# Second matmul and transposes as two 64-row array tiles, the upper half of each sum 1.5 steps behind the lower one

## The chip, the cores and the metric

One core of a Trainium2 chip runs the kernel. The metric is the device time of one execution in microseconds. The kernel before took 799.05 us (median of three runs, 798.12 to 799.97). Engine names are those of the profile: PE is the matrix engine and PEld its weight loads, DVE the vector engine, ACT the scalar engine, POOL and SP the two that issue transfers here.

## What is computed

A lightweight causal convolution (each of 8 heads has 7 softmax weights over time) is followed by a two-layer network with a leaky ReLU. Cut to what matters:

```python
# x: (8, 4096, 192)   weight: (8, 7)   w_in: (192, 2048)   w_out: (2048, 192)
w = softmax(weight, axis=-1)
y[b, s, c] = sum_k w[head(c), k] * x_padded[b, s + k, c]     # 6 zeros ahead of each row
h = y.reshape(32768, 192) @ w_in
g = maximum(0.01 * h, h)
out = g @ w_out                                              # (32768, 192), float32
```

## The kernel before, in words

**Tiling.** The 8 batch rows are taken in pairs. A *block* is 512 tokens of both rows of a pair, so there are 32 blocks (`NBLK`), and a block is worked on in 8 *steps* (`STEPS`). Two blocks are a *unit*, the piece that the convolution works on. The 192 channels are three chunks of 64 (`NCH`, `CH`); the two rows of a pair stand on partitions 0 to 63 and 64 to 127 of the same tiles.

**The stages of a block.** SP loads x; DVE casts it to bf16 (`cast_x`, L86); PE transposes it in 12 full 128x128 transposes (`transpose_x`, L98) into one tile `ptr` of two PSUM banks; DVE copies that out in one operation (`evac_x`, L110); the convolution is 21 DVE operations per unit (`conv_jobs`, L130 and L136), kept in the list `jobs` and handed out a few per step. The first matmul (`mm1`, L238) makes one tile `ph` of hidden values for each of 16 slices `f`: six pairs of matmuls over 64 rows and 512 columns, in each pair one on the lower and one on the upper 64 rows of the array, one batch row each. ACT turns each `ph` into bf16 hidden values `g` (L245). The second matmul (`mm2`, L256) adds 16 matmuls over all 128 rows and 192 columns into one sum for 128 tokens; two sums share a tile `po`, and DVE copies both out at once (`evac_o`, L268) for SP to store.

**What sets the order.** The order is written by hand (`manual_schedule`), and every engine runs its own list in that order. Step j of block b issues two `mm1` (12 matmuls, two ACT operations) and then the sum j of block b-1 (16 matmuls): the second matmul runs one block behind the first. At block b the steps j = 0, 1, 2 also cast, transpose and copy out x of block b+3. The convolution of unit u+1 is handed out while unit u is multiplied, from step 3 of the unit's first block on, two operations a step. The PSUM tiles are `ph` twice (two banks each), `po` twice (one bank each) and `ptr` once (two banks); the hidden values `g` have two buffers, the output tiles `o_sb` four.

**Names below.** A *pair* is two 64-row matmuls, one on the lower 64 rows of the array and one on the upper. An *even* block is the first of its unit (0, 2, 4 and so on).

## Time and profile before

| what | value |
|---|---|
| median of three runs | 799.05 us |
| the profiled execution, its own time | 798.81 us |
| its span, first to last instruction | 797.0 us |
| PE busy | 759.1 us, 95% |
| DVE, ACT busy | 517.2 us (65%), 506.6 us (64%) |
| first `mm2` matmul, last PE matmul ends | 57.03 us, 792.72 us |
| mean granted TensorE clock | 0.980 |

How to read it: the span is 1.8 us shorter than the execution's own time. A matmul's row gives its start and a length that overlaps the next one's, so the rate at which PE works is read from the distance of starts, not from the lengths. In the timeline a row is a run of equal instructions: its start, how long the run lasted, the engine, the line, the operation, how many, and in brackets the idle time before it with what ended that.

### The profile page before, as it was taken

To read this page: it belongs to the slowest core of one execution; us is meant where nothing else is said; L and a number is where in the kernel's file an instruction comes from. 1 tells how busy PE (TensorE), PEld (TensorE's weight loads), DVE (VectorE), ACT (ScalarE), POOL (GpSimd) and SP (SyncE) were. 2 spreads that over 40 slices of the span, in tenths; PEclk is the share of its full clock that TensorE was granted. 3 is DMA by queue.
4 is the path that set the end of the run, shared out by engine and by line. 5 is a ranking of instruction groups with operands and counts; after the bars stand their busy time and mean duration, and the time that the engine had idled before them with its cause. 6 is when DMAs were issued, how large, how long until landed. Compare 5 with 4: busy or idle time off the path is not lost.

```text
span 797.0 us, 16911 instructions
## 1 busy us (share of the span) xinstructions
PE 759.1 (95%) x7612; PEld 486.5 (61%) x7612; DVE 517.2 (65%) x592; ACT 506.6 (64%) x521; POOL 8.4 (1%) x19
## 2 busy tenths in 40 slices
PE   3299899999999999999999999999999999999997
PEld 3146566666666666666666666666666666666666
DVE  3889594766939476693947669394766939476011
ACT  1586466666666666666666666666666666666661
POOL 4000000000000000000000000000000000000000
PEclk9589899999999999999999999999999999999999
DMA  8910222212222211222221122222122221111111
GB/s 206 266 43 30 69 72 73 60 49 80 71 75 76 71 53 58 80 71 71 79 71 53 59 80 71 71 80 71 46 66 80 71 71 40 31 40 31 41 31 61
DMA packets 70097, 56.16 MB, mean 70 GB/s; under 512 B 3752, under 2 KB 69304, under 8 KB 69640
## 3 DMA queue, kind: packets, MB, share of 16 engines
q1 hardware_dynamic: 68608, 50.34, 20.9%
q0 software_dynamic: 1104, 4.73, 2.6%
q8 instruction: 59, 0.97, 0.5%
q14 instruction: 14, 0.11, 0.1%
q10 hardware_dynamic: 312, 0.01, 0.0%
HBM read 29.90 MB, written 25.17 MB: 69 GB/s over the span
## 4 chain that ended last, share of the span: by engine, by line
PE 89%; DVE 5%; DMA 3%; ACT 1%; issue 1%; POOL 0%; ACTq 0%; POOLq 0%
PE po L256 44%; PE ph L238 43%; DVE yt L136 4%; DMA w_stage<-in_moe_w_in_dram 3%; PE ptr L98 2%; ACT w_in L217 1%; DMA wk<-in_weight_dram 1%; DVE xt L110 0%; DVE o_sb L268 0%; DVE x_bf L86 0%; DVE yt L130 0%; ACT g L245 0%; POOL wk L156 0%; POOL w_stage L167 0%; POOL ident masks.py:199 0%
## 5 line engine op out<-in xcount | busy, mean ns | idle before, releaser
L245 ACT ACTIVATE g<-ph 128x1024 bf16<-128x1024 f32 x512 | 496.4, 1021 | 248.2 <-PE ph L238 248.1
L256 PEld LDWEIGHTS <-g 128*128 128x128 bf16 x4096 | 326.2, 98 | 105.8 <-issue 105.6
L238 PE MATMUL ph<-yt,w_in 64*128 64x512 bf16 x3072 | 381.5, 381 | 8.3 <-DVE yt L136 4.1
L256 PE MATMUL po<-w_out,g 128*128 128x192 bf16 x4096 | 382.2, 247 | 0.0
L136 DVE SCALAR_TENSOR_TENSOR yt<-xt,wk,yt 128x1024 bf16<-128x1024 bf16 (+1 forms) x306 | 373.4, 1220 | 8.7
L238 PEld LDWEIGHTS <-w_in 64*128 64x128 bf16 x3072 | 130.4, 94 | 173.5 <-issue 51.4
L268 DVE COPY o_sb<-po 128x384 f32<-128x384 f32 x128 | 71.1, 556 | 247.8 <-PE po L256 247.8
L98 PE MATMUL ptr<-ident,x_bf 128*128 128x128 bf16 x384 | 27.9, 225 | 17.1 <-DVE x_bf L86 17.1
L98 PEld LDWEIGHTS <-x_bf 128*128 128x128 bf16 x384 | 24.5, 101 | 18.5 <-DVE x_bf L86 17.2
L110 DVE COPY xt<-ptr 128x1536 bf16<-128x1536 bf16 x32 | 30.4, 951 | 7.4 <-PE ptr L98 5.8
L86 DVE CAST x_bf<-x_nat 128x768 bf16<-128x768 f32 x64 | 32.6, 552 | 0.0
L130 DVE TENSOR_SCALAR yt<-xt,wk 128x1024 bf16<-128x1024 bf16 (+1 forms) x51 | 23.7, 465 | 0.5
L217 ACT CAST w_in<-w_stage 128x1536 bf16<-128x1536 f32 x4 | 5.6, 1468 | 17.6 <-DMA w_stage<-in_moe_w_in_dram 17.6
L179 PE MATMUL warm<-ident 128*128 128x128 bf16 x60 | 6.0, 295 | 8.3 <-POOL ident masks.py:199 8.3
L179 PEld LDWEIGHTS <-ident 128*128 128x128 bf16 x60 | 5.8, 141 | 8.3 <-POOL ident masks.py:199 8.3
L187 DVE TENSOR_REDUCE nmax<-wk 128x3 f32<-128x21 f32 x1 | 0.2, 176 | 10.7 <-DMA wk<-in_weight_dram 10.7
L192 ACT ACT_TABLE_LOAD x1 | 1.3, 1283 | 7.8 <-DMA wk<-in_weight_dram 7.8
L156 POOL DMA_DIRECT2D wk<-in_weight_dram x10 | 5.3, 537 | 1.9 <-DMA wk<-in_weight_dram 1.1
L222 ACT CAST w_out<-wo_stage 128x3072 bf16<-128x3072 f32 x1 | 2.7, 2748 | 0.0
L192 ACT ACTIVATE wk<-wk,nmax 128x7 f32<-128x7 f32 x3 | 0.8, 302 | 1.8 <-DVE nmax L187 1.8
L167 POOL DMA_DIRECT2D w_stage<-in_moe_w_in_dram x2 | 1.3, 646 | 0.0
L172 POOL DMA_DIRECT2D wo_stage<-in_moe_w_out_dram x1 | 1.2, 1196 | 0.0
(11 smaller groups left out, 2.2 us busy)
## 6 DMA issues: line engine op xcount, KB each, us to landing
x_nat<-in_x_dram SPq DMA_DIRECT2D x64, 384.0 KB, 4.3
out_dram<-o_sb SPq DMA_DIRECT2D x128, 192.0 KB, 2.0
w_stage<-in_moe_w_in_dram POOLq DMA_DIRECT2D x2, 1536.0 KB, 16.9
wo_stage<-in_moe_w_out_dram POOLq DMA_DIRECT2D x1, 1536.0 KB, 25.3
wk<-in_weight_dram ACTq DMA_DIRECT2D x6, 0.7 KB
wk<-in_weight_dram POOLq DMA_DIRECT2D x6, 0.7 KB, 4.5
wk<-in_weight_dram ACTq DMA_DIRECT2D x2, 0.4 KB, 4.4
wk<-in_weight_dram ACTq DMA_DIRECT2D x2, 0.2 KB
```

The costliest lines, as they stand in the source:

```text
L86: nc.vector.tensor_copy(out=t[:, :, :, e, :], in_=x_nat[blk][:, e, :, :].rearrange("p s (c k) -> p s c k", c=NCH),)
L98: nc.tensor.transpose(out=t[:, c, s, :], in_=x_bf[blk][:, s, c, :, :].rearrange("p e k -> p (e k)"), identity=ident,)
L110: nc.vector.tensor_copy(out=xt[rp][:, :, HALO + st * ST : HALO + (st + 1) * ST], in_=ptr[blk][:, 0:NCH, :, :].rearrange("p c s t -> p c (s ...
L130: lambda s=src, d=dst, c=c: nc.vector.tensor_scalar_mul(d, s, wk[:, c, 0:1])
L136: lambda s=src, d=dst, c=c, k=k: nc.vector.scalar_tensor_tensor(out=d, in0=s, scalar=wk[:, c, k : k + 1], in1=d, op0=mybir.AluOpType.mult, ...
L156: eng.dma_start(out=wk[p : p + hi - lo, c, :], in_=weight[h : h + 1, :].to_broadcast((hi - lo, K)),)
L179: nc.tensor.matmul(out=wa[:, 0, 0:128], lhsT=ident, rhs=ident, start=(i == 0), stop=(i == 59),)
L217: nc.scalar.copy(out=w_in[:, :, q * (F // 4) : (q + 1) * (F // 4)], in_=w_stage[:, :, q * (F // 4) : (q + 1) * (F // 4)],)
L238: nc.tensor.matmul(out=ph[:, e, :], lhsT=w_in[ps, c, f * 128 : (f + 1) * 128], rhs=y[ps, c, ub * ST : (ub + 1) * ST], start=(c == 0), stop ...
L245: nc.scalar.activation(out=g[blk][:, f, :, :], in_=ph, func=mybir.ActivationFunctionType.Prelu, alpha=0.01,)
L256: nc.tensor.matmul(out=p[:, j % 2, :], lhsT=g[blk][:, fc, e, s * 128 : (s + 1) * 128], rhs=w_out[:, fc, :], start=(fc == 0), stop=(fc == N ...
L268: nc.vector.tensor_copy(out=o_sb, in_=po.pop((blk, q)))
```

## The change

The second matmul becomes pairs too. Each sum is split over the contraction: the lower 64 rows of `g` and `w_out` add 16 matmuls of 192 columns, the upper 64 rows another 16, and both halves add into the same `po` tile, which is now one sum wide and has a bank of its own. In step n the lower half of sum n is issued, alternating with upper-half matmuls that lag by `LAG` = 24 matmuls: first the last eight of sum n-2, then the first eight of sum n-1. A sum is therefore finished in the middle of the step two after its own, and is copied out there (`evac_o` with one sum of 192 columns instead of two). The first upper-half matmul of a sum is made to wait for the first ACT operation of the same step (`seal`). The last nine sums (from `LAST` on) are still made with 128 rows; before them come 24 upper-half matmuls without a partner.

The transposes become 24 transposes of 64 rows, alternating between the array's halves, into two tiles `ptr0` and `ptr1`. These and the `po` tiles now share one pool of four banks. `evac_x` is two copies. `g` has three buffers. The preparation of x runs one block further ahead (block b+4) at the steps 1 and 2, with the copies out right after the transposes and one convolution operation between; block 1 prepares two blocks. The convolution operations are spread evenly over the steps from step 0 of an even block.

PE where `mm1` ends and the second matmul begins; before (`ph` hidden values before ACT, `po` sums, `g` hidden values):

```order
L238 LDWEIGHTS w_in_255
L238 MATMUL ph_1511<-yt_927,w_in_255 128x512
L256 LDWEIGHTS g_1074
L256 MATMUL po_1485<-w_out_260,g_1074 128x192
L256 LDWEIGHTS g_1074
```

and now:

```order
L242 LDWEIGHTS w_in_280
L242 MATMUL ph_1448<-yt_511,w_in_280 128x512
L260 LDWEIGHTS g_982
L260 MATMUL po_1456<-w_out_285,g_982 128x192 [waits DVE_49]
L260 LDWEIGHTS g_515
L260 MATMUL po_1351<-w_out_285,g_515 128x192
```

The matmuls of two sums, from two blocks' hidden values here, now alternate, and the first of a new sum waits for DVE to have emptied its bank. In the middle of the same step the upper half changes over to the next sum:

```order
L260 LDWEIGHTS g_515
L260 MATMUL po_1351<-w_out_285,g_515 128x192
L260 LDWEIGHTS g_982
L260 MATMUL po_1456<-w_out_285,g_982 128x192
L260 LDWEIGHTS g_515 [waits Activation_49]
L260 MATMUL po_1403<-w_out_285,g_515 128x192
```

That weight load carries the new wait for ACT; nothing like it stood there before.

PE where the transposes begin in an even block; before:

```order
L256 LDWEIGHTS g_3204
L256 MATMUL po_3528<-w_out_260,g_3204 128x192
L98 LDWEIGHTS x_bf_3548 [waits DVE_49]
L98 MATMUL ptr_3585<-ident_114,x_bf_3548 128x128
L98 LDWEIGHTS x_bf_3548
```

and now:

```order
L260 LDWEIGHTS g_4165
L260 MATMUL po_4687<-w_out_285,g_4165 128x192
L101 LDWEIGHTS x_bf_4725 [waits DVE_49]
L101 MATMUL ptr0_4781<-ident_111,x_bf_4725 128x64
L101 LDWEIGHTS x_bf_4725
L101 MATMUL ptr1_4782<-ident_111,x_bf_4725 128x64 [waits DVE_49]
```

The first wait is for the cast, as before. The second is new: `ptr1` takes the bank of the sum that was finished in the middle of this same step, and waits for DVE's copy of it (the row `COPY o_sb_4763` below).

DVE at the begin of an even block, steps 0 to 2; before:

```order
L268 COPY o_sb_2613<-po_2547 128x384 [waits DMAHW1_49,PE_49]
L86 CAST x_bf_2636<-x_nat_2025 128x12x64 [waits DMAHW4_49]
L86 CAST x_bf_2636<-x_nat_2025 128x12x64 [waits DMAHW5_49]
L268 COPY o_sb_2700<-po_2616 128x384 [waits DMAHW4_49,PE_49]
L110 COPY xt_1810<-ptr_2671 128x3x512 [waits PE_49]
L130 TENSOR_SCALAR yt_2753<-xt_1810,wk_93 128x1024 [waits DVE_49]
```

and now:

```order
L303 COPY o_sb_4650<-po_4529 128x192 [waits DMAHW7_49,PE_49]
L134 TENSOR_SCALAR yt_4668<-xt_2082,wk_90 128x1024
L140 SCALAR_TENSOR_TENSOR yt_4668<-xt_2082,wk_90,yt_4668 128x1024 [waits DVE_49]
L303 COPY o_sb_4650<-po_4581 128x192 [waits PE_49]
L85 CAST x_bf_4725<-x_nat_3814 128x12x64 [waits DMAHW2_49]
L85 CAST x_bf_4725<-x_nat_3814 128x12x64 [waits DMAHW3_49]
L140 SCALAR_TENSOR_TENSOR yt_4668<-xt_2082,wk_90,yt_4668 128x1024 [waits DVE_49] x2
L303 COPY o_sb_4763<-po_4633 128x192 [waits DMAHW2_49,PE_49]
L140 SCALAR_TENSOR_TENSOR yt_4668<-xt_2082,wk_90,yt_4668 128x1024 [waits DVE_49]
L117 COPY xt_2082<-ptr0_4781 128x4x3x64 [waits PE_49]
```

The convolution now starts in step 0, and two casts and two convolution operations stand ahead of the copy in step 2 for which PE's second transpose waits.

The diff, cut to its core:

```diff
-    g_pool = ctx.enter_context(tc.tile_pool(name="g", bufs=2))
+    g_pool = ctx.enter_context(tc.tile_pool(name="g", bufs=3))
...
-    psum_o = ctx.enter_context(tc.tile_pool(name="po", bufs=2, space=bass.MemoryType.PSUM))
-    psum_tr = ctx.enter_context(tc.tile_pool(name="ptr", bufs=1, space=bass.MemoryType.PSUM))
+    psum_o = ctx.enter_context(tc.tile_pool(name="po", bufs=4, space=bass.MemoryType.PSUM))
...
     def transpose_x(blk):
-        t = psum_tr.tile([128, 4, SUB, 128], BF16, name="ptr")
+        ts = [psum_o.tile([128, SUB, NCH, CH], BF16, name=f"ptr{i}", tag="po") for i in range(2)]
         for s in range(SUB):
             for c in range(NCH):
...
+                for i in range(2):
+                    ps = slice(i * CH, (i + 1) * CH)
+                    nc.tensor.transpose(
+                        out=ts[i][:, s, c, :],
+                        in_=x_bf[blk][ps, s, c, :, :].rearrange("p e k -> p (e k)"),
+                        identity=ident[ps, ps],
+                    )
...
+        for i, t in enumerate(ptr.pop(blk)):
+            nc.vector.tensor_copy(out=dst[:, i], in_=t)
...
+    def mm2_one(rt, m, fc):
+        b, jj = divmod(m, STEPS)
+        e, s = divmod(jj, SUB)
+        if rt != 1 and fc == 0:
+            po[m] = psum_o.tile([128, D], FP32, name="po", tag="po")
+        ps = slice(0, 128) if rt is None else slice(rt * CH, (rt + 1) * CH)
+        ins = nc.tensor.matmul(
+            out=po[m],
+            lhsT=g[b][ps, fc, e, s * 128 : (s + 1) * 128],
+            rhs=w_out[ps, fc, :],
+            start=(rt != 1 and fc == 0),
+            stop=(rt != 0 and fc == NFC - 1),
+        )
+        if rt == 1 and fc == 0:
+            tc.add_manual_dep(
+                ins.ins, seal[m + 1],
...
+                reason="other row tile, same bank",
+            )
+
+    def mm2(n):
+        if n <= LAST:
+            for fc in range(NFC if n < LAST else LAG):
+                if n < LAST:
+                    mm2_one(0, n, fc)
+                t1 = n * NFC + fc - LAG
+                if t1 >= 0:
+                    mm2_one(1, *divmod(t1, NFC))
+                    if t1 % NFC == NFC - 1:
+                        evac_o(t1 // NFC)
+        if n >= LAST:
+            for fc in range(NFC):
+                mm2_one(None, n, fc)
+            if n < NBLK * STEPS - 1:
+                evac_o(n)
...
+    LAG = NFC + NFC // 2
+    LAST = (NBLK - 1) * STEPS - 1
...
         if j == at + 1:
             transpose_x(blk)
-        if j == at + 2:
+            run_jobs(1)
             evac_x(blk)
...
+            elif blk == 1:
+                prep(4, j, 0)
+                prep(5, j, 4)
             else:
-                prep(blk + 3, j, 0)
-            if ub == 0 and j == (7 if blk == 0 else 3) and unit + 1 < NUNIT:
+                prep(blk + 4, j, 1)
+            if ub == 0 and j == (7 if blk == 0 else 0) and unit + 1 < NUNIT:
                 jobs += conv_jobs(unit + 1, [(0, UT)])
...
+            left = (7 - j) if blk == 0 and j < 7 else (UB - ub) * STEPS - j
+            run_jobs(-(-len(jobs) // left))
```

## The prediction

> **What bounds the kernel now.** I read the page first: busy shares and the chain that ended last.

> ```profile
> PE 759.1 (95%) x7612; PEld 486.5 (61%) x7612; DVE 517.2 (65%) x592; ACT 506.6 (64%) x521; POOL 8.4 (1%) x19
> ...
> PE 89%; DVE 5%; DMA 3%; ACT 1%; issue 1%; POOL 0%; ACTq 0%; POOLq 0%
> ```

> PE is the bound, and nothing else comes near. The question is whether it could do its matmuls in less time. So next the timeline of one step in mid-run, and of the end, where only second matmuls are left:

> ```profile
> 400.22 1.47 PE L238 MATMUL ph<-yt,w_in 64*128 64x512 bf16 x12
> ...
> 401.08 1.94 ACT L245 ACTIVATE g<-ph 128x1024 bf16<-128x1024 f32 x2 [0.89 <-PE ph L238]
> ...
> 401.62 1.27 PEld L256 LDWEIGHTS <-g 128*128 128x128 bf16 x16 [0.42 <-issue]
> 401.62 1.49 PE L256 MATMUL po<-w_out,g 128*128 128x192 bf16 x16
> ...
> 403.05 0.39 PE L238 MATMUL ph<-yt,w_in 64*128 64x512 bf16 x2
> ...
> 780.67 12.05 PE L256 MATMUL po<-w_out,g 128*128 128x192 bf16 x144
> 782.20 0.56 DVE L268 COPY o_sb<-po 128x384 f32<-128x384 f32 x1 [5.09 <-PE po L256]
> ```

> The groups by shape give the mean length of one, by which distances of starts follow from runs:

> ```profile
> L245 ACT ACTIVATE g<-ph 128x1024 bf16<-128x1024 f32 x512 | 496.4, 1021 | 248.2 <-PE ph L238 248.1
> L256 PE MATMUL po<-w_out,g 128*128 128x192 bf16 x4096 | 382.2, 247 | 0.0
> L238 PE MATMUL ph<-yt,w_in 64*128 64x512 bf16 x3072 | 381.5, 381 | 8.3 <-DVE yt L136 4.1 <-ACT g L245 3.8
> ...
> L98 PE MATMUL ptr<-ident,x_bf 128*128 128x128 bf16 x384 | 27.9, 225 | 17.1 <-DVE x_bf L86 17.1
> ```

> A step lasts 403.05 - 400.22 = 2.83 us. In the closing run 144 matmuls start every (12.05 - 0.25) / 143 = 0.0825 us. In the first matmul six pairs start every (1.47 - 0.38) / 5 = 0.218 us; I use 0.216, since the first distance holds a little of the changeover. Undisturbed, a step would take 6 x 0.216 + 16 x 0.0825 = 1.294 + 1.320 = 2.614 us. The missing 0.214 us lies where the line changes: 1.40 us from 400.22 to 401.62 and 1.43 from there on, each 0.11 too long. At the first the weight load idles 0.42 us with its semaphores met ("issue"). A change between 64-row and 128-row matmuls costs 0.107 us here, twice a step.

> **The change part by part.** *Pairs in the second matmul.* Both changeovers go. What a pair of 192 columns costs is not in the trace: from below 0.0825 us, one full matmul's time, from above two of them in turn, 0.165. I take 0.0825, by the nearest row: a pair of L238 starts every 0.216 us and not every two times that, so two halves do run side by side. A pair needs two weight loads where there was one. A warm run of transposes, which have a load each, bounds a load:

> ```profile
> 50.71 0.84 PE L98 MATMUL ptr<-ident,x_bf 128*128 128x128 bf16 x12
> ```

> (0.84 - 0.22) / 11 = 0.056 us for matmul and load, and both tiles' loads fit into 0.0825 us if they overlap at all, as those of L238 seem to.

> [...]

> The steps that can gain are those from block 2 on (block 1 waits for DVE, below): 239 second matmuls x 0.214 = **-51.1 us**.

> *The new wait for ACT.* The load of each sum's first upper half waits for the first ACT operation of the step, and all of PE's list waits behind it. When would it come? ACT starts 401.08 - 400.22 = 0.86 us after the first matmul, less 0.01 without a changeover, and lasts 1.02: it ends at 1.87 in the step. How long PE takes to see that:

> ```profile
> 46.03 1.94 ACT L245 ACTIVATE g<-ph 128x1024 bf16<-128x1024 f32 x2
> ...
> 47.11 0.39 PE L238 MATMUL ph<-yt,w_in 64*128 64x512 bf16 x2 [0.20 <-ACT g L245]
> ```

> The first of these ACT operations ends at 46.03 + 1.02 = 47.05, the matmul starts at 47.11: 0.06 us. Release at 1.93; the ninth pair is due at 1.294 + 8 x 0.0825 = 1.954. It holds by 0.02 us: **0**. From above, if the pair had to wait for a whole load of 0.10 us after the release, 0.07 us x 247 = +17 us.

> *The transposes.* A pair of 64 columns: from below half of 0.056, from above twice. I take 0.056, no change (24 loads remain, in pairs): **0**, with -9 to +19 us over 28 blocks as ends.

> *The wait of `ptr1` for DVE.* It needs DVE's prices:

> ```profile
> 55.75 0.48 DVE L130 TENSOR_SCALAR yt<-xt,wk 128x1024 bf16<-128x1024 bf16 x1
> 56.26 2.60 DVE L136 SCALAR_TENSOR_TENSOR yt<-xt,wk,yt 128x1024 bf16<-128x1024 bf16 x2
> 58.78 1.02 DVE L86 CAST x_bf<-x_nat 128x768 bf16<-128x768 f32 x2
> 59.72 3.92 DVE L136 SCALAR_TENSOR_TENSOR yt<-xt,wk,yt 128x1024 bf16<-128x1024 bf16 x3
> ...
> 400.60 0.55 DVE L268 COPY o_sb<-po 128x384 f32<-128x384 f32 x1
> 401.06 2.60 DVE L136 SCALAR_TENSOR_TENSOR yt<-xt,wk,yt 128x1024 bf16<-128x1024 bf16 x2
> ```

> From start to start: the scalar product 0.51, two fused operations 2.52 (1.32 and 1.20), two casts 0.94, a copy of 384 columns 0.46. A copy of 192 I put at 0.27, between half of that and all of it; its result is there 0.09 later (0.55 - 0.46). A copy begins 0.29 us after the last matmul of its sum has started: 782.20 against 780.67 + 15 x 0.0825 = 781.91. The upper half of a sum ends with the eighth pair, so its copy can begin at 1.294 + 7 x 0.0825 + 0.29 = 2.16 us in the step.

> In an even block, from its begin: step 0's copy at 2.16, then the scalar product and one fused operation, free at 4.14. Step 1's copy at 2.61 + 2.16 = 4.77 to 5.04, casts to 5.98, two fused operations to 8.50. Step 2's copy is due at 7.38 and starts at 8.50; PE sees its end at 8.50 + 0.36 + 0.06 = 8.92. PE has finished step 2's pairs at 3 x 2.614 = 7.84 and stands for 1.08 us. The blocks are 2, 4 to 26: 13 x 1.08 = **+14.0 us**. In an odd block one scalar product takes the place of the two fused operations; the copy comes on time, is seen at 7.38 + 0.42 = 7.80, and PE passes. The ends: 0, and twice that if the odd blocks wait too.

> *The start.* Block 2 cannot begin before DVE has convolved unit 1:

> ```profile
> 83.65 1.46 PE L238 MATMUL ph<-yt,w_in 64*128 64x512 bf16 x6 [4.13 <-DVE yt L136]
> ...
> 42.70 0.96 DVE L110 COPY xt<-ptr 128x1536 bf16<-128x1536 bf16 x1 [3.08 <-PE ptr L98]
> 43.57 0.74 DVE L136 SCALAR_TENSOR_TENSOR yt<-xt,wk,yt 128x512 bf16<-128x512 bf16 x1
> ```

> PE idled 4.13 us for it, so what block 1 gains on PE is lost, and DVE's list decides. It gets longer: at 42.70 DVE already waits 3.08 us for transposes, and now two fused operations of 0.75 fewer stand before that wait (+1.5); block 1 casts and copies out one block more (0.94, and two copies that I put at a cast's 0.47 each: +1.9); six copies of 0.27 replace three of 0.46 (+0.2). Block 2 starts **+3.6 us** later.

> *The end.* 24 upper halves without a partner, 24 x 0.0825 = **+2.0 us**; the last copy is half as wide, **-0.2**.

> *What costs nothing.* 128 more copies on DVE (from 71 to some 70 to 90 us in all, beside 517 of 797 us busy), the third `g` buffer and the earlier loads lie under PE. Without that cover a step of two fused operations and a copy, 2.52 + 0.27 = 2.79, is longer than 2.61; with one or two in turn DVE catches up. PE's wait for an empty bank at the begin of the second matmul comes 1.29 us into the next step, 1.34 us after step 1's copy is seen at best (3.91 against 2.57), which even the late copies of an even block keep.

> Sum: -51.1 + 14.0 + 3.6 + 2.0 - 0.2 = -31.7 us. The profiled execution's own time was 798.81, so 767.1, and the median of 799.05 stands 0.24 above it: I say **767 us**.

> **The rivals.** *The wait for ACT bites.* ACT's end is seen 0.02 us before the ninth pair; if that pair's restart costs as much as a changeover, 0.107 us, each step gives half its gain back: 247 x 0.107 = 26 us, **793 us**. For it speaks how thin the margin is; against it, that 47.11 shows PE going on with two matmuls and three loads at once after such a wait.

> *The even blocks do not wait.* If DVE's operations run ahead of my count, 14 us less: **753 us**. The count speaks against it, as the order is fixed and PE faster.

> *Slower: the loads of the two halves come one after the other.* One mechanism on PE: a pair needs two loads, and if each takes the 0.056 us that a transposing load with its matmul takes, a pair starts every 0.112 us. Then 16 x 0.112 = 1.79, the step 3.08 us, 0.47 over the forecast's: 247 x 0.47 = +116, less the 14 us of even blocks, since DVE then keeps up: **869 us**. It turns to a loss as soon as a pair costs over 0.0825 + 0.214 / 16 = 0.096 us. [...] Against it, 12 loads of L238 in a step hide behind matmuls; but at 0.216 us a pair there is room for it, so they cannot exclude it.

> *It does not do what it says:* the halves run in turn at 0.165 us, 247 x 1.32 = +326 over the forecast, some **1080 us**. The pairs of L238 speak against it.

> **How the numbers follow.** The forecast 0.60; ACT 0.17; no waits 0.10; the loads 0.10; in turn 0.03. The range of the likeliest: transposes -9 to +19, even blocks -14 to +14, ACT's end 0 to +17, pulled together to 752 to 788. To leave out no more than two tenths it reaches on to the case of ACT: **752 to 798**. A change under 0.2%, some 1.6 us, cannot be told from none. Faster are the first three cases, 0.87, of which I give 0.01 to no change, with 0.01 from the slower ones; slower 0.12. So 0.86, 0.02, 0.12.

> **What would show it.** In the profile after: runs of pairs in which the second matmul follows the first without the 0.42 us of "issue", and a step of 2.61 us; a row in which transposes wait for `o_sb` about 1.1 us, 13 times; a wait of the first matmul at block 2 on DVE that ends near 87 us; no wait of the second matmul's loads on ACT worth naming. A step over 2.7 us would make the prediction wrong, by ACT if a wait of PE names it, by the loads if PE is busy throughout.

## The result and the profile after

| | before | after |
|---|---|---|
| median | 798.97 us (798.12 to 799.97, four runs) | 758.74 us (757.79 to 759.85, four runs) |
| ratio | | 0.950 (95% interval 0.948 to 0.952) |
| profiled execution, its span | 798.81 us, 797.0 us | 757.87 us, 756.1 us |
| PE's wait for DVE at block 2 ends | 83.65 us | 86.54 us |

The change is worth 40 us. The forecast was 767 us, in a range of 752 to 798: right in sign and inside the range, 8 us too slow. The page of the changed kernel, its busy shares and the chain that ended last:

```profile
PE 700.1 (93%) x11948; PEld 565.5 (75%) x11948; DVE 520.3 (69%) x752; ACT 506.6 (67%) x521; POOL 8.5 (1%) x19
...
PE 81%; DVE 11%; DMA 3%; issue 3%; ACT 1%; POOL 0%; ACTq 0%; POOLq 0%
```

PE is still the bound, but DVE has taken 11% of the chain where it had 5%. PE has 57% more instructions than before (11948 against 7612) and is busy 59 us less. Now an even block of the changed kernel in the timeline, its steps 2 and 3 (columns: start, length of the run, engine, line, operation, how many, and the idle time ahead of it):

```profile
399.84 0.19 PE L101 MATMUL ptr<-ident,x_bf 64*128 64x64 bf16 x1
400.56 0.35 DVE L303 COPY o_sb<-po 128x192 f32<-128x192 f32 x1
...
400.97 0.51 PE L101 MATMUL ptr<-ident,x_bf 64*128 64x64 bf16 x23 [0.89 <-DVE o_sb L303]
...
401.30 1.47 PE L242 MATMUL ph<-yt,w_in 64*128 64x512 bf16 x12
...
402.63 1.50 PE L260 MATMUL po<-w_out,g 64*128 64x192 bf16 x32
...
403.94 1.47 PE L242 MATMUL ph<-yt,w_in 64*128 64x512 bf16 x12
404.81 1.94 ACT L249 ACTIVATE g<-ph 128x1024 bf16<-128x1024 f32 x2 [0.71 <-PE ph L242]
...
405.24 1.50 PE L260 MATMUL po<-w_out,g 64*128 64x192 bf16 x32
...
406.56 0.40 PE L242 MATMUL ph<-yt,w_in 64*128 64x512 bf16 x2
```

Three things stand there. From 403.94 to 406.56 a step lasts 2.62 us, where it was 2.83: the first matmul takes 405.24 - 403.94 = 1.30 us, the second 1.32, and neither has the 0.11 us at the change of lines any more. At 399.84 one transpose starts and the second stands until 400.97, for the copy that ran from 400.56. And 23 transposes then take only 401.30 - 400.97 = 0.33 us until the next matmul.

All waits of PE in the changed kernel (in total, how often, the longest):

```profile
PE ptr L101 <- DVE x_bf L85: 17.3, 2, 17.1
PE ptr L101 <- DVE o_sb L303: 13.0, 14, 1.4
...
PE ph L242 <- ACT g L249: 4.9, 6, 3.5
PE ph L242 <- DVE yt L140: 4.8, 3, 2.7
PE po L260 <- DVE xt L117: 3.0, 1, 3.0
```

The second row is new; one of its 14 waits belongs to the start (1.45 us), the other 13 to the even blocks. The second matmul waits for ACT only once: the loads' own row for that, `PEld L260 <- ACT g L249`, holds 0.3 us in one piece. The start and an odd block, in the timeline:

```profile
86.54 1.04 PE L242 MATMUL ph<-yt,w_in 64*128 64x512 bf16 x8 [2.67 <-DVE yt L140]
...
88.72 1.51 PE L242 MATMUL ph<-yt,w_in 64*128 64x512 bf16 x12
...
116.34 0.54 PE L101 MATMUL ptr<-ident,x_bf 64*128 64x64 bf16 x23
116.69 0.38 PE L242 MATMUL ph<-yt,w_in 64*128 64x512 bf16 x1
```

Block 2 begins 2.89 us later than before. In the odd block nothing waits, and 24 transposes hold the list for 116.69 - 116.34 = 0.35 us.

The sum of the prediction has no term for one thing that stands at the begin of block 2. In the kernel before, the step after the one that waited began here:

```profile
88.15 1.66 PE L238 MATMUL ph<-yt,w_in 64*128 64x512 bf16 x12
```

After its wait of 4.13 us, PE needed 88.15 - 83.65 = 4.50 us for the eight matmuls and the sum that were left of that step, where its other steps leave 2.83 - 2 x 0.216 = 2.40 us; the granted clock was 0.50 in these 4.50 us and 0.62 over the 6.4 us from 83.65 on. The profiled execution of the changed kernel went on at a clock of 1.00 after its 2.67 us and needed 88.72 - 86.54 = 2.18 us, what its other steps leave. With the step behind it, 0.2 us too long before, that makes 2.3 us. They cannot be put down to the change: behind the same wait of 2.67 us at this place, the kernel of the completed table below took 87.97 - 86.61 = 1.36 us for the eight matmuls, and the changed kernel 87.40 - 86.54 = 0.86. What decides it is not shown.

**The sum, settled.** The two profiled executions differ by 40.94 us. A block of eight steps without transposes, from its first matmul to the next block's, takes 22.61 us before and 20.92 after, 0.21 a step; 239 steps: -50.2. The 13 waits cost 400.97 - 399.84 less the 0.03 at which the second transpose was due, 1.10 us each: +14.3. The start: +2.9, and -2.3 for the clock after it. Twenty-six blocks transpose in 0.35 us each, where twenty-seven took 12 x 0.056 = 0.67: -9.0 (block 5 now does it at the start, under a wait for DVE). Two late releases that come once each, by ACT in block 17 and by the convolution in block 30: +1.0. The upper halves without a partner and the last copy: +1.9. Together -41.4, 0.5 us more than measured, which is less than two runs of one kernel differ.

### The profile page after: what moved, and what is told of

Same layout as the page of the kernel before. It is cut to its first block, busy times and chain, and to the rows that moved or that the text cites. A ratio compares the mean times of both kernels' runs of the same rounds, so it can differ in the third digit from the quotient of the medians.

```text
span 756.1 us, 25743 instructions
## 1 busy us (share of the span) xinstructions
PE 700.1 (93%) x11948; PEld 565.5 (75%) x11948; DVE 520.3 (69%) x752; ACT 506.6 (67%) x521; POOL 8.5 (1%) x19
## 4 chain that ended last, share of the span: by engine, by line
PE 81%; DVE 11%; DMA 3%; issue 3%; ACT 1%; POOL 0%; ACTq 0%; POOLq 0%
PE po L260 40%; PE ph L242 39%; DVE yt L140 7%; DMA w_stage<-in_moe_w_in_dram 3%; DVE x_bf L85 2%; PE ptr L101 2%; DVE o_sb L303 1%; ACT w_in L221 1%; DMA wk<-in_weight_dram 1%; DVE xt L117 1%; ACT w_out L226 0%; ACT g L249 0%; DVE yt L134 0%; POOL wk L160 0%; POOL w_stage L171 0%
## 5 line engine op out<-in xcount | busy, mean ns | idle before, releaser
L249 ACT ACTIVATE g<-ph 128x1024 bf16<-128x1024 f32 x512 | 496.4, 1021 | 204.9 <-PE ph L242 204.9
L260 PEld LDWEIGHTS <-g 64*128 64x128 bf16 (+1 forms) x8048 | 364.1, 94 | 47.2 <-issue 4.2
L242 PE MATMUL ph<-yt,w_in 64*128 64x512 bf16 x3072 | 388.7, 379 | 10.0 <-ACT g L249 4.9
L260 PE MATMUL po<-w_out,g 64*128 64x192 bf16 (+1 forms) x8048 | 391.6, 243 | 3.1 <-DVE xt L117 3.0
L242 PEld LDWEIGHTS <-w_in 64*128 64x128 bf16 x3072 | 195.9, 95 | 97.0 <-issue 17.8
L303 DVE COPY o_sb<-po 128x192 f32<-128x192 f32 x256 | 90.9, 355 | 209.8 <-PE po L260 209.8
L101 PE MATMUL ptr<-ident,x_bf 64*128 64x64 bf16 x768 | 20.4, 193 | 30.3 <-DVE x_bf L85 17.3
L101 PEld LDWEIGHTS <-x_bf 64*128 64x128 bf16 x768 | 17.4, 97 | 33.6 <-DVE x_bf L85 17.9
L117 DVE COPY xt<-ptr 128x768 bf16<-128x768 bf16 x64 | 32.4, 547 | 7.0 <-PE ptr L101 7.0
```

The source lines that it names most:

```text
L101: nc.tensor.transpose(out=ts[i][:, s, c, :], in_=x_bf[blk][ps, s, c, :, :].rearrange("p e k -> p (e k)"), identity=ident[ps, ps],)
L117: nc.vector.tensor_copy(out=dst[:, i], in_=t)
L242: nc.tensor.matmul(out=ph[:, e, :], lhsT=w_in[ps, c, f * 128 : (f + 1) * 128], rhs=y[ps, c, ub * ST : (ub + 1) * ST], start=(c == 0), stop ...
L249: return nc.scalar.activation(out=g[blk][:, f, :, :], in_=ph, func=mybir.ActivationFunctionType.Prelu, alpha=0.01,)
L260: ins = nc.tensor.matmul(out=po[m], lhsT=g[b][ps, fc, e, s * 128 : (s + 1) * 128], rhs=w_out[ps, fc, :], start=(rt != 1 and fc == 0), stop ...
L303: nc.vector.tensor_copy(out=o_sb[:, n % 2, :], in_=po.pop(n))
```

## The experiments

The theory after this result: the gain is the two changeovers of a step; the even blocks give 14 us of it back, because a copy of DVE stands behind convolution; transposes in halves are worth some 8 us more; ACT's end lies just ahead of the pair that needs it. The rivals: the step got shorter for another reason than the changeovers; the list is no longer in DVE's hand, so that an even spread costs nothing; the alternating order, rather than the split, does the work.

Times below are medians. The kernel before, run beside them, took 797.9 to 798.5 us.

### The price of a changeover: one 128-row matmul in each step, and the same with 64 rows

Into each step comes one matmul of 64 columns at the begin of the second matmul. It writes into the new sum's bank, and the sum's first matmul overwrites it. Once it has 128 rows:

```diff
-        if rt != 1 and fc == 0:
+        if rt is None and fc == 0:
...
+            if n < LAST:
+                b, jj = divmod(n, STEPS)
+                e, s = divmod(jj, SUB)
+                po[n] = psum_o.tile([128, D], FP32, name="po", tag="po")
+                nc.tensor.matmul(
+                    out=po[n][:, 0:CH],
+                    lhsT=g[b][0:128, 0, e, s * 128 : (s + 1) * 128],
+                    rhs=w_out[0:128, 0, 0:CH],
+                    start=True,
+                    stop=True,
+                )
```

> The changed kernel with one matmul more in each step, ahead of the second matmul: 128 rows, 64 columns, into the new sum's bank, overwritten by the sum's first matmul. Theory (a change between 64-row and 128-row matmuls costs 0.107 us): 0.027 + 2 x 0.107 = 0.24 us a step, 239 x 0.24 = 58, less 6 since the even blocks wait 2 x 0.24 less: 810 us. Rival (the 0.21 us a step of the kernel before lay in something else that changed with the line, as the bank or the operands): 0.027 a step, 765 us.

The control reads `0:CH` in place of `0:128`, twice, so that the matmul stays in 64-row form.

> The same with 64 rows for the one matmul more, the control. Theory: no change of tile size, 0.027 us a step less 0.7 us of even blocks' waits: 764 us. Rival: if it costs as much as the 128-row one, 810 us, the changeover isn't the cause.

With 128 rows 811.52 us, with 64 rows 762.93. Both timelines, first the 128 rows:

```profile
498.73 1.46 PE L242 MATMUL ph<-yt,w_in 64*128 64x512 bf16 x12
500.12 0.20 PE L286 MATMUL po<-w_out,g 128*128 128x64 bf16 x1
500.25 1.49 PE L260 MATMUL po<-w_out,g 64*128 64x192 bf16 x32
501.58 1.46 PE L242 MATMUL ph<-yt,w_in 64*128 64x512 bf16 x12
```

and the 64 rows:

```profile
501.71 1.50 PE L242 MATMUL ph<-yt,w_in 64*128 64x512 bf16 x12
503.00 0.24 PE L260 MATMUL po<-w_out,g 64*128 64x192 bf16 x1
503.05 0.19 PE L286 MATMUL po<-w_out,g 64*128 64x64 bf16 x1
503.07 1.48 PE L260 MATMUL po<-w_out,g 64*128 64x192 bf16 x31
504.35 1.50 PE L242 MATMUL ph<-yt,w_in 64*128 64x512 bf16 x12
```

A step lasts 501.58 - 498.73 = 2.85 us with the 128-row matmul and 504.35 - 501.71 = 2.64 with the 64-row one. The same columns cost 0.03 us in the one form and 0.24 in the other. The 0.10 us before L286 (500.12 - 498.73 = 1.39 where the control has 503.00 - 501.71 = 1.29) and the 0.13 behind it, in which its own 0.03 lies, are the two changeovers. 247 steps x 0.21 = 52 us, less 3.8 us that the waits of the even blocks shrink (12.0 to 8.2 us): 48, where the two medians differ by 48.6. The changeover explains the step by itself; the rival, by which the 128-row form would cost no more than the other, is out by 46 us. A change costs 0.10 to 0.11 us here; what PE does in that time no row of these traces tells.

### Undo the pairs of the second matmul

```diff
-    LAST = (NBLK - 1) * STEPS - 1
+    LAST = 0
```

Every sum is made with 128 rows again; all else of the change stays.

> The changed kernel with every sum made by 16 matmuls of 128 rows, as before the change; the transposes in halves, the order of the preparation and of the convolution stay. Theory: the two changeovers come back, 239 x 0.214 = +51 us; the waits of the even blocks go, since a sum is finished in its own step, -14; no halves without a partner, -2: 794 us. Rival (the gain comes from the shorter transposes, the third g buffer and the evenly spread convolution): 765 us or less.

794.49 us, ratio 0.996 (0.994 to 0.998). The step is 2.83 us again, from 502.27 to 505.10, and the idle time of the weight loads at the change is back, in the waits of this kernel:

```profile
PEld L260 <- issue: 106.1, 248, 0.8
```

248 times 0.43 us is the 0.42 that the prediction read in one step. What is left of the change, half-row transposes, smaller copies and the new spread of DVE's work, comes to 3.4 us in sum: some 9 us of shorter transposes, less a block 2 that begins 4.0 us later than in the kernel before (87.67 against 83.65). The pairs carry the rest.

### The two halves one after the other, and in groups of eight

First 16 lower halves and then 16 upper ones, with the same lag and waits:

```diff
-            for fc in range(NFC if n < LAST else LAG):
-                if n < LAST:
+            if n < LAST:
+                for fc in range(NFC):
                     mm2_one(0, n, fc)
+            for fc in range(NFC if n < LAST else LAG):
                 t1 = n * NFC + fc - LAG
```

> The changed kernel with the same 32 half matmuls in each step, but the 16 lower ones first and the upper ones after them, not alternating. Theory (the two halves run side by side only where they alternate in PE's list): 32 x 0.0825 = 2.64 us instead of 1.32, 247 x 1.32 = +326, less the 14 us of even blocks: 1071 us. Rival (PE takes matmuls of the other half ahead of those that wait): no slower than 770 us.

922.79 us, from one run. Both expectations are missed, by some 150 us each: the step is 504.83 - 501.51 = 3.32 us in the rows below, where halves strictly in turn give 1.294 + 32 x 0.0825 = 3.93. PE's timeline of this kernel:

```profile
501.51 0.33 PE L260 MATMUL po<-w_out,g 64*128 64x192 bf16 x2
...
503.52 0.39 PE L242 MATMUL ph<-yt,w_in 64*128 64x512 bf16 x1
503.60 0.33 PE L260 MATMUL po<-w_out,g 64*128 64x192 bf16 x2
503.75 0.38 PE L242 MATMUL ph<-yt,w_in 64*128 64x512 bf16 x1
503.76 0.24 PE L260 MATMUL po<-w_out,g 64*128 64x192 bf16 x1
...
504.83 0.33 PE L260 MATMUL po<-w_out,g 64*128 64x192 bf16 x2
```

In the list all 32 of L260 stand ahead of the next step's L242. Yet a matmul of L242 starts at 503.52, and three of L260 behind it, at 503.60, 503.68 and 503.76. So a matmul for the lower half of the array starts ahead of the last three that are listed before it for the upper half. The time saved against halves in turn is 3.93 - 3.32 = 0.61 us over two changes (lower to upper, upper to the next step): as an estimate from these steps 0.61 / 2 / 0.0825 = 3.7 matmuls at each.

In groups of eight, four matmuls side by side at each change would fill both halves. With the 3.7 of this run in place of the "some four" of the expectation below, by the same estimate each of the four changes of a step (lower to upper twice, upper to lower, upper to the next step) would cost 0.3 x 0.0825 = 0.025 us, 0.10 us a step.

```diff
-            for fc in range(NFC if n < LAST else LAG):
-                if n < LAST:
-                    mm2_one(0, n, fc)
+            half = NFC // 2
+            for rt, fc in [
+                (rt, fc)
+                for o in range(0, NFC if n < LAST else LAG, half)
+                for rt in (0, 1)
+                for fc in range(o, o + half)
+            ]:
```

> The changed kernel with the halves in groups of eight: eight lower matmuls, eight upper, and so again, instead of one by one. In the run with 16 in turn PE lost 0.70 us a step instead of 1.32, and upper matmuls began while about four lower ones were still to start. Theory (PE looks some four matmuls ahead, each half keeping its own order): groups of eight then overlap without a gap in either half, the sum is finished 0.33 us later, as with a lag of 28: 763 to 768 us. Rival (it looks ahead only at the change of line, or in the order of the list): each step 0.3 to 1.3 us longer, 830 us or more.

781.83 us, again between the two, but nearer the theory: the step is 2.69 us. Both ends of one step in the timeline, the second with the change ahead of it:

```profile
497.86 1.24 PE L242 MATMUL ph<-yt,w_in 64*128 64x512 bf16 x9
...
500.23 0.39 PE L242 MATMUL ph<-yt,w_in 64*128 64x512 bf16 x1
500.30 0.32 PE L260 MATMUL po<-w_out,g 64*128 64x192 bf16 x2
500.45 0.38 PE L242 MATMUL ph<-yt,w_in 64*128 64x512 bf16 x1
500.47 0.24 PE L260 MATMUL po<-w_out,g 64*128 64x192 bf16 x1
500.55 1.24 PE L242 MATMUL ph<-yt,w_in 64*128 64x512 bf16 x9
```

500.55 - 497.86 = 2.69, some 0.07 above the alternating order. Over the four changes of the step that is 0.018 us each, by the same estimate 4 - 0.018 / 0.0825 = 3.8 matmuls side by side at each: the two runs agree. Both show the same picture at the change to the next step: when the first matmul of the lower half starts (500.23 here, 503.52 above), three earlier listed ones of the upper half are still to start (500.30 to 500.47 here, 503.60 to 503.76 above). The second one of the lower half follows after 0.22 us here and 0.23 above, where a pair takes 0.216 elsewhere. Why it is three and not four is not shown.

239 x 0.07 = 17 of the 23 us. By the distances between the first matmuls of successive blocks, the 13 odd blocks are 0.2 us and the 13 even ones 0.1 us longer still than eight such steps make them, 4 us in sum; there the sum is finished later in its step, and its copy too. What makes up the rest is not shown.

### Transposes of 128 rows put back

```diff
-        ts = [psum_o.tile([128, SUB, NCH, CH], BF16, name=f"ptr{i}", tag="po") for i in range(2)]
+        ts = [psum_o.tile([128, 2, NCH, 128], BF16, name=f"ptr{i}", tag="po") for i in range(2)]
...
-                for i in range(2):
-                    ps = slice(i * CH, (i + 1) * CH)
-                    nc.tensor.transpose(
-                        out=ts[i][:, s, c, :],
-                        in_=x_bf[blk][ps, s, c, :, :].rearrange("p e k -> p (e k)"),
-                        identity=ident[ps, ps],
-                    )
+                nc.tensor.transpose(
+                    out=ts[s // 2][:, s % 2, c, :],
+                    in_=x_bf[blk][:, s, c, :, :].rearrange("p e k -> p (e k)"),
+                    identity=ident,
+                )
...
```

Twelve transposes, six into each of the two banks. The copies out are fitted to the new layout.

> The changed kernel with 12 transposes of 128 rows and columns in place of the 24 halves, into the same two banks. Theory: each block gets two changeovers, 0.21 us, and 12 x 0.056 = 0.67 us of transposes instead of 0.35: +0.53 x 26 = +14 us; in the even blocks the second bank is needed 0.45 us later, so the wait there shrinks by 13 x 0.45 = 6: 767 us. Rival (transposes lie beside other work and their form does not matter): 753 to 759 us.

765.56 us, 6.8 above the change. The six behind the wait, and the line after them:

```profile
491.46 0.51 PE L99 MATMUL ptr<-ident,x_bf 128*128 128x128 bf16 x6
492.42 0.50 PE L99 MATMUL ptr<-ident,x_bf 128*128 128x128 bf16 x6 [0.45 <-DVE o_sb L301]
492.85 1.47 PE L240 MATMUL ph<-yt,w_in 64*128 64x512 bf16 x12
```

From 492.42 to 492.85 are 0.43 us for six and the changeover back, 6 x 0.056 + 0.107 = 0.44. So a block costs 0.32 us more by the transposes and 0.21 by the changeovers, 26 x 0.53 = 14 us. Since six transposes now run before the bank is needed, the 13 waits shrink from 0.89 to 0.45 us, 6 us back: 8 us worked out, 6.8 measured. Most of what the half-row transposes save in the even blocks is thus time that PE would otherwise have used while waiting.

### The lag

```diff
-    LAG = NFC + NFC // 2
+    LAG = 22
```

The upper half changes to its new sum two pairs earlier, with the seventh pair, and waits there for the same ACT operation.

> The changed kernel with the upper half 22 matmuls behind instead of 24, so that the new sum's first upper half is due at pair 7 instead of pair 9, at 1.79 us in the step. Theory (PE's whole list waits for ACT's end, seen at 1.93): 0.14 us a step, 239 x 0.14 = 34, less 4 of shorter waits in even blocks: 789 us. Rival (only the upper half waits and the lower goes on): 756 to 760 us.

787.56 us. The row of its waits in which the loads wait for ACT:

```profile
PEld L260 <- ACT g L249: 46.6, 228, 0.5
```

and one step in its timeline:

```profile
499.85 1.53 PE L242 MATMUL ph<-yt,w_in 64*128 64x512 bf16 x12
...
500.77 1.94 ACT L249 ACTIVATE g<-ph 128x1024 bf16<-128x1024 f32 x2 [0.82 <-PE ph L242]
...
501.14 1.71 PE L260 MATMUL po<-w_out,g 64*128 64x192 bf16 x32
501.85 0.77 PEld L260 LDWEIGHTS <-g 64*128 64x128 bf16 x19 [0.20 <-ACT g L249]
...
502.61 0.46 PE L242 MATMUL ph<-yt,w_in 64*128 64x512 bf16 x2
```

The ACT operation ends at 500.77 + 1.02 = 501.79, the load goes at 501.85, 0.06 later as the prediction read. The step is 2.76 us, 0.14 longer: two pairs earlier is 0.165, and the wait is that less the margin, so the margin of the change is about 0.02 us. So the gain rests on little: were the first ACT operation of each step to end later than that, each step should give the excess back. No run moves ACT itself.

With `LAG = 28` the first upper half comes four pairs later, and each sum is finished four pairs later too.

> The upper half 28 matmuls behind: the wait for ACT has 0.33 us more room, and each sum is finished four pairs, 0.33 us, later. Theory (that wait costs nothing now; the even blocks wait for the copy of the sum): nothing gained at ACT. In even blocks DVE, not the sum, is late, so their wait stays or grows by up to 0.33; in odd blocks the copy is seen 0.29 us after PE is ready: +4 to +8 us, 763 to 767 us. Rival (ACT's end costs a little in each step now): 750 us or less.

767.26 us, 8.5 more. Steps without transposes stay at 2.62 us, so there was no wait for ACT left to remove. The copy comes later and the even blocks' wait grows, and now the odd blocks hold the line as well:

```profile
117.36 0.80 PE L101 MATMUL ptr<-ident,x_bf 64*128 64x64 bf16 x24
117.99 1.47 PE L242 MATMUL ph<-yt,w_in 64*128 64x512 bf16 x12
...
493.04 0.19 PE L101 MATMUL ptr<-ident,x_bf 64*128 64x64 bf16 x1
494.44 0.51 PE L101 MATMUL ptr<-ident,x_bf 64*128 64x64 bf16 x23 [1.21 <-DVE o_sb L303]
```

13 x (1.21 - 0.89) + 13 x (117.99 - 117.36 - 0.35) = 4.2 + 3.6 = 7.8 us. Of the three lags 24 is the smallest that does not wait for ACT, and the larger one only delays the copies.

### DVE's work handed out around the copy

The theory says that the even blocks wait since convolution stands ahead of the copy in step 2. So from block 2 on a table sets how many operations each step hands out, with none in the step of the casts:

```diff
+    PLAN = ((2, 0, 0, 2, 1, 2, 1, 2), (2, 0, 0, 2, 1, 2, 2, 0))
...
-            run_jobs(-(-len(jobs) // left))
+            run_jobs(-(-len(jobs) // left) if blk < 2 else PLAN[ub][j])
```

In blocks 28 and 29, where nothing more is prepared, this table hands out two operations too few. All of them still run (270 wide ones, as in the change), but the last two of the last unit only in block 30: that block's first step is multiplied without those two weights of the third chunk, and its next step waits for DVE.

> The changed kernel with the convolution operations handed out by a table from block 2 on: none in the step of the casts, none after the transposes' copies, one or two elsewhere, the same 21 per unit. Theory (PE's wait in 13 even blocks comes from the two operations ahead of step 2's copy): the 13 waits of 1.08 us go, 758.7 - 14 = 745 us, no row of transposes waiting for o_sb but that of block 1. Rival (DVE's work is only moved, and its backlog meets PE elsewhere, at an empty bank or in the odd blocks): 755 to 760 us, with a wait of the second matmul for DVE in its place.

745.66 us; PE waits for `yt` 6.1 us here, three times. With the two operations put back to where they belong:

```diff
+            run_jobs(-(-len(jobs) // left) if blk < 2 else PLAN[ub][j] + (j == 2 and blk + 4 >= NBLK))
```

> The table of the earlier run with the last unit's two operations put back (that table left them out, in blocks 28 and 29, where no preparation hands them out). Theory: 13 waits of 1.08 us gone as there, two operations of 1.3 us on DVE more in blocks whose DVE has room: 745 us. Rival (part of the 13 us came from the operations left out): 748 us or more.

743.03 us, ratio to before 0.930 (0.928 to 0.932), 15.7 us below the change. PE's waits in this kernel:

```profile
PE ptr L101 <- DVE x_bf L85: 18.0, 2, 17.1
...
PE ph L242 <- DVE yt L140: 4.3, 2, 2.7
```

The row of `o_sb` is gone, and nothing has come in its place; `yt` stands at 4.3 us in two waits, which is 1.8 of the 2.6 us by which this kernel is ahead of the first table. Of the 15.7 us, the 13 waits explain 13 x 1.10 = 14.3; the late convolution in block 30, 0.7 us, is gone as well. DVE has the same 752 operations, busy 524.3 us where the change has 520.3; only their order differs. The rival, that another wait would take their place, is out.

### The start

On top of that table, block 5 is prepared in block 2 instead of block 1, three convolution operations instead of one stand ahead of block 2's copies out, and blocks 2 and 3 have a table of their own:

```diff
-            run_jobs(1)
+            run_jobs(3 if blk == 2 else 1)
...
-                prep(5, j, 4)
+            elif blk == 2:
+                prep(5, j, 0)
+                prep(6, j, 4)
...
```

> The same, and a shorter way to block 2: block 5 is prepared in block 2 instead of block 1, and in block 0 three operations instead of one stand ahead of DVE's first wait for transposes. Theory (block 2 starts when DVE has convolved unit 1): 1.9 and 1.5 us less on DVE, 742 us, the first matmul of block 2 near 83 us. Rival (the wait of the second matmul for its bank in block 1, 3.0 us, or the transposes set the start): 745 us.

740.66 us (738.46 to 741.38), ratio to before 0.927 (0.925 to 0.929). The begin of block 2:

```profile
82.42 0.82 PE L242 MATMUL ph<-yt,w_in 64*128 64x512 bf16 x6 [2.93 <-DVE yt L140]
```

It comes 4.1 us earlier than in the change, and 1.2 earlier than in the kernel before; the profiled executions of the two tables differ by 3.8 us, the medians by 2.4. This kernel is 18 us faster than the change and 58 faster than the kernel before.

## Why the prediction was right, and where it was off

**The changeovers, right.** "A change between 64-row and 128-row matmuls costs 0.107 us here, twice a step": the step fell by 0.21 us, the control pair puts 48.6 us on putting the change back, and undoing the pairs gives 2.83 us again.

**A pair in 0.0825 us, right.** The step needs no other number. The two slow rivals, loads one after the other (869 us) and halves in turn (1080 us), are both refuted by 405.24 to 406.56 us: 16 pairs in 1.32 us. The case of 1080 us is out even where the list invites it: 16 halves listed after 16 others cost 164 us and not 326, and at 503.52 us of that run a matmul starts ahead of three listed before it. Two weight loads of 128 columns go with each of these pairs, every 0.0825 us in the second matmul, and every 0.33 / 11.5 = 0.029 us in the transposes. How long one load lasts by itself these distances do not show.

**ACT's end, right by a hair.** Seen at 1.93 against 1.954, the prediction gave it 0 with 0.17 for the other case. A lag of 22 shows the wait at once; its size puts the margin near 0.02 us, as worked out. With rows read to 0.01 us such a margin could hardly be told from none beforehand, so that it held was in part luck.

**The wait for the copy, right.** "13 x 1.08": it came 13 times, with 1.10 us each. The table that takes it away gives 15.7 us.

**The transposes, mis-sized.** "I take 0.056, no change (24 loads remain, in pairs)". A transposing pair takes 0.029 us: the lower end of the bounds. In 26 blocks that is 8.3 of the 9.2 us between the sum (767.1) and the profiled execution (757.87); the prediction's bounds counted 28. The other differences nearly cancel: the clock at block 2, the start and a block transposed at the start against steps that gained 0.21 and not 0.214 and two late releases. The step that failed is the choice between the ends: the row of full transposes was taken as nearest, in which 0.056 us go with 128 columns; a half-row transpose has 64. What the first matmul's rows showed was not applied here: a pair of 512 columns starts every 0.216 us, about the 512 / 192 x 0.0825 = 0.22 us that one alone is estimated at, and the 12 loads of six pairs take 0.98 us beside the 1.47 us of the matmuls.

**The start, a little too dear.** Said +3.6, measured +2.9; the mechanism and its place, DVE's list ahead of block 2, are as said: the wait ended at 86.54 us for the "near 87". That the kernel before lost 2.3 us behind its own wait, at a granted clock of 0.62 over 6.4 us, and this execution of the changed one, at 1.00, did not, the prediction did not see; with it the start costs 0.6 us in all.

**What "costs nothing" cost nothing**: no wait of PE names the `g` buffers, the x loads or the wider row of copies. The second matmul waits for an empty bank once, 3.0 us in block 1 (`PE po L260 <- DVE xt L117`), where block 2's wait for DVE follows anyway. One exception appears once, 0.55 us near 697 us, where a first matmul waits for convolution.

## What to carry to other kernels

Where a kernel alternates between matmuls that use half of the array's rows and matmuls that use all of them, look for an idle time of the weight loads at the change with all semaphores met (0.42 us here), and count the changes: splitting the full ones over the contraction into two halves, listed alternately, cost nothing in rate here and gave 0.21 us per round back. When PE's steps get shorter, count every other engine's list anew at the places where buffers are shared, since over a quarter of the gain was lost here to one copy that stood behind work that nobody waited for, and a table of how many operations each step hands out brought it back. Between bounds far apart, take the one whose mechanism already shows in a neighbouring row, not the one whose operation has the same name.
